# Gate and value of two more blocks by a seven-product scheme, with running sums carried between PSUM banks by ScalarE

## The chip, the cores and the metric

The kernel runs on one core of a Trainium2 chip. Its engines work side by side, each through its own queue, in the order of that queue: TensorE (PE: matmuls; PEld: its weight loads), VectorE (DVE), ScalarE (ACT), GpSimd (POOL) and SyncE (SP), which here issues the DMAs. The metric is the device time of one execution in microseconds (us); of the kernel before there are three runs, with a median of 913.91 us (913.44 to 915.89).

## The reference

Three stages follow each other on 2304 tokens of 512 numbers, all in fp32: attention within a window of 64 positions (4 sequences of 576, 8 heads of 64), then two gated feed-forward layers of width 1536. Cut to what is computed:

```python
attn = softmax(mask(q @ k.T / 8)) @ v          # rel in [0, 64)
x = attn.transpose(0, 2, 1, 3).reshape(2304, 512)
xn = x / sqrt(mean(x * x) + 1e-6) * rms_g      # layer 1
g = xn @ w_gate
x1 = (g * sigmoid(g) * (xn @ w_val)) @ w_out
gate = sigmoid(x1 @ w2_gate)                   # layer 2
out = (gate * (x1 @ w2_val)) @ w2_out
```

## The kernel before

**Tiles.** The tokens are cut into six blocks of 384 (`BLOCKS`). The width 1536 is cut into 12 groups `f` of 128, two of which share one weight tile: the tiles 0 to 11 of a layer are gate and value in turn, 12 to 17 are `w_out`. Each fp32 matrix is multiplied as three fp16 matmuls (high by high, high by low, low by high), and weights and activations are therefore split into a high and a low half first: ScalarE writes the high half, VectorE the low one (`w_split`, L312; `rms_split`, L543; `moe_h`, L598). The weights come in by 1 MB DMAs (`w_load`), their largest value is found (`w_max`, L237), they are converted (`w_conv`, L264 to L266) and split (L327, L329).

**Layer 1** (`l == 0` in the code) goes block by block and group by group: `moe_g` and `moe_v` each put 12 matmuls of 128x384 into one bank (L567; 4 slices of the 512 inputs, 3 matmuls each), `moe_h` splits the product, and `moe_o` (L627 to L629) adds its 12 matmuls to four banks of the output. Blocks 0 and 1 share a first stretch in which the weights are still being prepared; blocks 2 to 5 follow, each with its attention and its normalisation placed ahead of it by `place`.

**Layer 2** (`l == 1`) takes two blocks as a pair and uses Strassen's scheme in Winograd's form for gate and value. The inputs are seen as a 2x2 matrix of quadrants (two halves of the 512 inputs, two blocks) and the weights as one of 2x2 quadrants. Seven products of six matmuls (`product`, L737) take the place of eight. The sums of weight quadrants are made by `w_sums` (L303), the sums of input quadrants by `xform_items` (L696). In `moe_w` (L743) the results are put together: ScalarE copies one product out of its bank (L752), VectorE makes five additions with L741, each reading a bank, and two further products are added by TensorE itself into a bank that holds a product already. The output matmuls are L633 to L635.

**Order.** Every instruction gets a priority from `at` and `place`; the final order on each engine is then fixed by `arrange` (L1086) from a packed table, `ORDER` (L1041), with the scheduler's dependencies kept as semaphore waits. PSUM has eight banks: 0 to 3 hold outputs, 4 and 5 serve `moe_g` and `moe_v`, 4 to 7 serve `moe_w` (`BANKS_OF`).

## Time and profile before

| | |
|---|---|
| median of three runs | 913.91 us |
| the profiled execution, its own time | 915.78 us |
| its span, first to last instruction | 914.0 us |
| PE busy | 886.4 us (97%) |
| DVE busy | 634.2 us (69%) |
| ACT busy | 394.6 us (43%) |
| mean granted TensorE clock | 0.981 |

Busy time is the time in which an engine has an instruction under way. The span is 1.78 us shorter than the profiled execution's own time, which is 1.87 us above the median. By the timeline the matmuls of layer 1 begin at 51.86 us, the last matmuls of layer 1 and the first steps of layer 2 lie around 523 us, and the last matmul starts at 909.46 us.

### The profile page before, as it was taken

How to read it: one execution, taken by the hardware profiler on the slowest of the kernel's cores; microseconds unless marked ns; L12 is line 12 of the kernel's file. 1: busy time of each engine (PE TensorE's matmuls, PEld its weight loads, DVE VectorE, ACT ScalarE, POOL GpSimd, SP SyncE). 2: the span in 40 equal slices, each digit the busy share in tenths (PEclk: the TensorE clock that was granted, in tenths of full speed). 3: DMA queues.
4: the chain of work that ended last, by engine and by line, in shares of the span. 5: the costliest groups of instructions: out<-in, count | busy, mean ns of one | idle time of the engine just before them, and what ended most of it. 6: DMA issues, size and time to landing. Idle time of an engine off the chain costs nothing.

```text
span 914.0 us, 14970 instructions
## 1 busy us (share of the span) xinstructions
PE 886.4 (97%) x6120; PEld 527.9 (58%) x6120; DVE 634.2 (69%) x1209; ACT 394.6 (43%) x834; POOL 28.4 (3%) x37
## 2 busy tenths in 40 slices
PE   4699999999999999999999999999999999999998
PEld 3566665666666666666666655555555555555543
DVE  6999999798887689446789788657454644534440
ACT  5867546456553544432363554234223331323220
POOL 0000000000010001001000000000000000000000
PEclk7689999999999999999999999999999999999999
DMA  8752634312322163100021211000010000000001
GB/s 318 244 207 104 237 133 156 128 52 81 122 98 82 54 209 148 37 24 1 1 93 47 93 47 47 1 1 1 1 47 1 1 12 1 24 24 24 1 24 58
DMA packets 18789, 68.11 MB, mean 75 GB/s; under 512 B 2208, under 2 KB 2592, under 8 KB 13600
## 3 DMA queue, kind: packets, MB, share of 16 engines
q1 hardware_dynamic: 18720, 67.15, 20.5%
q8 instruction: 48, 0.79, 0.4%
q14 instruction: 21, 0.17, 0.1%
HBM read 62.43 MB, written 4.72 MB: 73 GB/s over the span
## 4 chain that ended last, share of the span: by engine, by line
PE 83%; DVE 11%; DMA 4%; issue 1%; ACT 1%; SPq 0%; POOL 0%; ACTq 0%
PE bank L737 27%; PE bank L567 23%; PE bank L635 5%; PE bank L634 5%; PE bank L633 5%; PE bank L627 4%; PE bank L629 4%; PE bank L628 4%; DVE wl L329 2%; PE bank L472 2%; DMA wl<-in_moe_w_val_dram 2%; PE bank L435 2%; DVE wmax L237 2%; DMA wl<-in_moe_w_gate_dram 1%; PE bank L402 1%; DVE wl L266 1%
## 5 line engine op out<-in xcount | busy, mean ns | idle before, releaser
L567 PE MATMUL bank<-xhl,wl 128*128 128x384 f16 x1728 | 297.3, 326 | 1.5 <-DVE th L581 1.1
L567 PEld LDWEIGHTS <-wl 128*128 128x128 f16 x1728 | 167.8, 98 | 112.1 <-issue 3.6
L737 PEld LDWEIGHTS <-wl 128*128 128x128 f16 x1512 | 148.0, 98 | 108.3
L737 PE MATMUL bank<-att,wl 128*128 128x384 f16 x1008 | 176.1, 326 | 0.0
L579 ACT ACTIVATE th<-bank,tg 128x384 f32<-128x384 f32 x72 | 41.6, 578 | 102.9 <-PE bank L567 68.8
L741 DVE TENSOR_TENSOR xhl<-xhl,bank 128x384 f32<-128x384 f32 x74 | 40.7, 552 | 61.3 <-PE bank L737 56.3
L627 PE MATMUL bank<-hh,wl 128*128 128x384 f16 x192 | 62.7, 326 | 0.0
L628 PE MATMUL bank<-hh,wl 128*128 128x384 f16 x192 | 62.6, 326 | 0.0
L629 PE MATMUL bank<-hh,wl 128*128 128x384 f16 x192 | 62.6, 326 | 0.0
L327 ACT ACTIVATE wl<-wl,isc 128x1024 f16<-128x1024 f32 (+1 forms) x42 | 48.5, 1162 | 17.2 <-DVE isc L246 10.2
L581 DVE SCALAR_TENSOR_TENSOR th<-th,bank 128x384 f32<-128x384 f32 x72 | 39.4, 548 | 22.6 <-ACT th L579 22.3
L592 DVE SCALAR_TENSOR_TENSOR th<-th,bank 128x384 f32<-128x384 f32 x72 | 39.4, 547 | 13.9 <-PE bank L567 13.3
L237 DVE TENSOR_REDUCE wmax<-wl 128x1 f32<-128x1024 f32 x36 | 43.6, 1213 | 5.5 <-DMA wl<-in_moe_w_val_dram 2.7
L264 ACT ACTIVATE wl<-wl 128x1024 f32<-128x1024 f32 x36 | 41.1, 1148 | 12.8 <-PE bank L567 3.7
L737 PE MATMUL bank<-wl 128*128 128x384 f16 x252 | 45.5, 326 | 0.0
L737 PE MATMUL bank<-wl,wl 128*128 128x384 f16 x252 | 45.4, 326 | 0.0
L418 ACT ACTIVATE sm<-sm,nm 128x128 f32<-128x128 f32 x96 | 37.3, 391 | 17.8 <-DVE nm L412 17.6
L633 PE MATMUL bank<-wl,xhl 128*128 128x512 f16 x111 | 42.1, 379 | 0.0
L634 PE MATMUL bank<-wl,xhl 128*128 128x512 f16 x111 | 42.1, 379 | 0.0
L635 PE MATMUL bank<-wl,xhl 128*128 128x512 f16 x111 | 42.1, 379 | 0.0
L629 PEld LDWEIGHTS <-wl 128*128 128x128 f16 x288 | 28.2, 98 | 18.8 <-DVE wl L329 0.2
L627 PEld LDWEIGHTS <-wl 128*128 128x128 f16 x288 | 28.2, 98 | 18.4 <-issue 1.0
(246 smaller groups left out, 1305.8 us busy)
## 6 DMA issues: line engine op xcount, KB each, us to landing
wl<-in_moe_w_out_dram SPq DMA_DIRECT2D x15, 1024.0 KB, 4.9
wl<-in_moe_w_val_dram SPq DMA_DIRECT2D x13, 1024.0 KB, 4.9
wl<-in_moe_w_gate_dram SPq DMA_DIRECT2D x12, 1024.0 KB, 5.0
vn<-in_v_dram SPq DMA_DIRECT2D x27, 256.0 KB, 3.5
att<-in_k_dram SPq DMA_DIRECT2D x13, 384.0 KB, 5.6
att<-in_q_dram SPq DMA_DIRECT2D x17, 256.0 KB, 5.2
out_dram<-vn SPq DMA_DIRECT2D x12, 256.0 KB, 2.1
out_dram<-sm SPq DMA_DIRECT2D x6, 256.0 KB, 2.3
```

Of the source, the lines that this page charges most:

```text
L237: V.tensor_reduce(out=r1[:, i:i + 1], in_=wraw(layer, j + i)[:, :, 1].bitcast(F32), axis=AX.X, op=ALU.max, apply_absolute_value=True)
L264: A.activation(out=y.bitcast(F32), in_=hi.bitcast(F32), func=AF.Prelu, scale=2.0 ** -112, alpha=-2.0 ** 32)
L327: A.activation(out=hi, in_=y, func=AF.Copy, scale=sc)
L567: T.matmul(pb[:, 0:n], lhsT=w_, rhs=x_, start=(c == 0), stop=(c == m - 1))
L579: A.activation(out=th[:, 0:n], in_=pg[:, 0:n], func=AF.Tanh, scale=sc)
L627: T.matmul(o[c][:, 0:n], lhsT=wh[:, cs], rhs=hi, start=st, stop=False)
L628: T.matmul(o[c][:, 0:n], lhsT=wh[:, cs], rhs=lo, start=False, stop=False)
L629: T.matmul(o[c][:, 0:n], lhsT=wl[:, cs], rhs=hi, start=False, stop=en)
L633: T.matmul(o[t], lhsT=h[:, 0, ts_], rhs=wh, start=st, stop=False)
L634: T.matmul(o[t], lhsT=h[:, 0, ts_], rhs=wl, start=False, stop=False)
L635: T.matmul(o[t], lhsT=h[:, 1, ts_], rhs=wh, start=False, stop=en)
L737: T.matmul(pb[:, 0:NMAX], lhsT=w_, rhs=x[:, t, kk], start=first and c == 0, stop=c == 5, skip_group_check=not first)
```

## The change

Blocks 4 and 5 of layer 1 (`PAIRED`) become a pair like those of layer 2: six steps `("W", 0, 2, s)` of seven products for gate and seven for value stand where 24 calls each of `moe_g` and `moe_v` stood, and the matmuls of L567 for them, 2 blocks x 12 groups x 24 matmuls = 576, become 6 steps x 2 x 7 products x 6 matmuls = 504. For it:

- the normalised blocks 4 and 5 stay in fp32 (no `rms_split`; the multiplication of 128x1536 in `rms_scale`, L541, becomes four of 128x384 that take the gain in), and `xform_items(0, 2)` makes their seven sums: four subtractions of 128x768 on VectorE, seven splits of 128x768 on both engines;
- the sums of layer 1's weight quadrants are made from the split weights, per tile: the high and low half are added back (`s_sum`, 128x1024), then the four sums of 128x256, then two splits (`s_hi`, `s_lo`), for 12 tiles;
- seven weight tiles of layer 2 (4 to 10) are now loaded twice: once early for `w_max`, once again for conversion; in all 47 instead of 40 weight loads.

In both layers `moe_w` puts the results together in another way: each gate or value of a step has three ScalarE copies (L809 after; two of them from one bank to another, where the following product is added on top) and two VectorE additions, where it had one copy and five additions.

```diff
+PAIRED = (4, 5)
...
+    def s_sum(s, m):
+        x, d = s_raw(m), wdst(0, 2 * s + m)
+        V.tensor_tensor(out=x[:, :, 1], in0=d[:, 0:1024], in1=d[:, 1024:2048], op=ALU.add)
+
+    def s_hi(s, m):
+        x, d, r = s_raw(m), wdst(0, 2 * s + m), s_form(s, m)
+        A.activation(out=r[:, 0:768], in_=x[:, 0:768, 0], func=AF.Copy, scale=0.25)
+        A.activation(out=d[:, 768:1024], in_=x[:, 768:1024, 1], func=AF.Copy, scale=0.25)
+
+    def s_lo(s, m):
+        x, d, r = s_raw(m), wdst(0, 2 * s + m), s_form(s, m)
+        V.scalar_tensor_tensor(out=r[:, 768:1536], in0=x[:, 0:768, 0], scalar=0.25, in1=r[:, 0:768], op0=ALU.mult, op1=ALU.subtract)
+        V.scalar_tensor_tensor(out=d[:, 1792:2048], in0=x[:, 768:1024, 1], scalar=0.25, in1=d[:, 768:1024], op0=ALU.mult, op1=ALU.subtract)
...
-            a = bank("w")
-            product(a, p, s, m, 0, 0, True)
+            def go(pb, a, b, first=False):
+                product(pb, l, p, s, m, a, b, first)
+
+            def copy(o, i):
+                A.activation(out=o[:, 0:NMAX], in_=i[:, 0:NMAX], func=AF.Copy)
+
+            a, e = bank("w"), bank("w")
+            go(a, 0, 0, True)
+            go(e, 6, 6, True)
             b = bank("w")
-            product(b, p, s, m, 5, 5, True)
-            u2 = take()
-            A.activation(out=u2, in_=a[:, 0:NMAX], func=AF.Copy)
-            add(u2, u2, b[:, 0:NMAX])
-            d = bank("w")
-            product(d, p, s, m, 4, 4, True)
-            u4 = take()
-            add(u4, u2, d[:, 0:NMAX])
-            e = bank("w")
-            product(e, p, s, m, 6, 6, True)
-            c22 = take()
-            add(c22, u4, e[:, 0:NMAX])
-            product(a, p, s, m, 1, 1, False)
...
+            copy(b, a)
+            go(b, 5, 5)
+            go(a, 1, 1)
+            c = bank("w")
+            copy(c, b)
+            go(c, 4, 4)
+            go(b, 2, 3)
+            x22, x21 = take(), take()
+            copy(x21, e)
+            add(x22, x21, c)
+            add(x21, x21, b)
+            go(c, 3, 2)
...
-    for b in range(DEFER, SKEW):
+    for b in range(DEFER, PAIRED[0]):
         gv(0, b, range(FC))
+    for s in range(NG):
+        main.append(("W", 0, 2, s))
+        if s:
+            oo(0, 4, [2 * s - 2, 2 * s - 1])
+    oo(0, 4, [10, 11])
+    oo(0, 5, range(FC))
...
 ORDER = (
-    'c-n1N2S8L;x}I~+T!yJkp$srX9~i(vdKG;tDE35*i7_VGly#p<Of-4xiZO9bdD$eIP1I+i8>6nSCbo?lD=P-22#6?k=pCfPG^X71MwuDz9h`E@DgQbD_'
+    'c-n1O30zdw{-57Dckb*A+pzDTvV$m~prB?V8foS7K9yVKQam*=%Oy*nOSzS%zWmeQ>`Cg&J#me+z%X+|kj;feLH5-FhFR`C@3PFyy<@YTbI<x)zQ6D9H'
```

The table `ORDER` is new from its first entry on. Three places of it follow; the names are tiles with their buffer number and the program's number, and a bracket names the engine or DMA queue whose semaphore is waited for.

**The start, on VectorE.** Before, from its third instruction; `nm` is a maximum of the attention scores, `wmax` that of a weight tile:

```order
L409 TENSOR_REDUCE nm_0_142<-bank_0_122 128x4 [waits PE_49]
L409 TENSOR_REDUCE nm_0_142<-bank_1_123 128x4 [waits PE_49]
L414 TENSOR_SCALAR nm_0_142<-nm_0_142 128x8 [waits DVE_49]
L265 TENSOR_SCALAR wl2_74<-wl2_74 128x1024 [waits DMAHW3_49]
L237 TENSOR_REDUCE wmax_0_390<-wl2_74 128x1
L270 TENSOR_REDUCE gam_0_114<-rg_77 128x1 [waits DMAHW6_49]
L266 SCALAR_TENSOR_TENSOR wl2_74<-wl1_73,wl2_74 128x1024 [waits DVE_49,Activation_49]
L192 TENSOR_SCALAR pgam_79<-gamr_0_116 128x1 [waits Pool_49]
L193 TENSOR_SCALAR pgam_79<-pgam_79 128x1 [waits DVE_49]
L409 TENSOR_REDUCE nm_1_180<-bank_2_160 128x4 [waits PE_49]
```

After:

```order
L412 TENSOR_REDUCE nm_0_143<-bank_0_123 128x4 [waits PE_49]
L412 TENSOR_REDUCE nm_0_143<-bank_1_124 128x4 [waits PE_49]
L417 TENSOR_SCALAR nm_0_143<-nm_0_143 128x8 [waits DVE_49]
L412 TENSOR_REDUCE nm_1_181<-bank_2_161 128x4 [waits PE_49]
L412 TENSOR_REDUCE nm_1_181<-bank_3_162 128x4 [waits PE_49]
L417 TENSOR_SCALAR nm_1_181<-nm_1_181 128x8 [waits DVE_49]
L238 TENSOR_REDUCE wmax_0_391<-wl2_74 128x1 [waits DMAHW5_49]
L266 TENSOR_SCALAR wl2_74<-wl2_74 128x1024
L422 TENSOR_SCALAR su_0_144<-su_0_144 128x8 [waits Activation_49]
```

The scores of the second pair (`nm_1`) come ahead of the first weight tile, whose `w_max` comes ahead of its conversion. SP issues the second pair's `k` and `q` ahead of the first weight tile too, where they came behind it.

**ScalarE, around the end of layer 1.** Before, in block 5's gate and value (L579 is the tanh of `moe_g`, L608 the high half of `moe_h`, L264 and L327 conversion and split of weights, L752 the copy and L781 the tanh of the first step of layer 2):

```order
L608 ACTIVATE hh_2_2311<-th_1_535 128x384 [waits DVE_49]
L752 ACTIVATE th_0_469<-bank_6_209 128x384 [waits DVE_49,Activation_49]
L579 ACTIVATE th_2_605<-bank_4_197,tg1_84 128x384 [waits PE_49]
L264 ACTIVATE wl1_73<-wl2_74 128x1024 [waits DMAHW5_49,PE_49]
L608 ACTIVATE hh_3_2399<-th_2_605 128x384 [waits DVE_49,PE_49]
L702 ACTIVATE wl1_73<-xhl_2_326,sx_1_5592 128x768
L781 ACTIVATE hh_0_2161<-bank_6_209,be_0_4910 128x384 [waits DVE_49,PE_49]
L327 ACTIVATE wl1_73<-wl2_74,isc_83 128x1024 [waits DVE_49]
```

After, in the paired blocks (L809 is the copy, L832 the tanh, L759 and L760 are the two lines of `s_hi`):

```order
L809 ACTIVATE bank_7_211<-bank_4_198 128x384 [waits DVE_49,PE_49]
L832 ACTIVATE vn_1_359<-hh_3_2394,tgs_87 128x384 [waits DVE_49,Activation_49]
L832 ACTIVATE th_1_536<-bank_5_204,tgs_87 128x384 [waits PE_49]
L759 ACTIVATE wl2_74<-wl2_74 128x768 [waits DVE_49]
L330 ACTIVATE wl1_73<-wl2_74,isc_83 128x768
L809 ACTIVATE bank_5_204<-bank_7_211 128x384 [waits DVE_49,PE_49]
L330 ACTIVATE wl1_73<-wl2_74,isc_83 128x1024
L809 ACTIVATE hh_3_2394<-bank_6_210 128x384 [waits DVE_49,PE_49,Activation_49]
L760 ACTIVATE wl1_73<-wl2_74 128x256 [waits DVE_49]
L809 ACTIVATE bank_4_198<-bank_6_210 128x384 [waits DVE_49,PE_49]
```

Four copies, three of them between banks, stand between splits of weights that wait for VectorE.

**ScalarE, in layer 2, where the second pair begins.** Before (L790 is the split of the gated product, L702 that of an input sum):

```order
L752 ACTIVATE th_0_469<-bank_6_209 128x384 [waits DVE_49,PE_49]
L790 ACTIVATE th_2_605<-wl2_74,hs2_88 128x384 [waits DVE_49]
L790 ACTIVATE xhl_1_263<-xhl_1_263,hs2_88 128x384 [waits DVE_49]
L781 ACTIVATE wl2_74<-wl2_74,be_0_4910 128x384
L781 ACTIVATE wl2_74<-bank_6_209,be_1_5613 128x384 [waits PE_49,Activation_49]
L752 ACTIVATE xhl_1_263<-bank_7_210 128x384 [waits PE_49]
L702 ACTIVATE att_76<-xhl_3_521,sx_2_6329 128x768
```

After (L809 the copy, L832 the tanh, L850 the split, L708 that of an input sum):

```order
L832 ACTIVATE xhl_2_327<-bank_4_198,be_1_5728 128x384 [waits PE_49]
L809 ACTIVATE bank_4_198<-bank_6_210 128x384 [waits PE_49,Activation_49]
L832 ACTIVATE xhl_3_522<-bank_5_204,be_1_5728 128x384 [waits PE_49]
L809 ACTIVATE bank_5_204<-bank_4_198 128x384 [waits PE_49,Activation_49]
L832 ACTIVATE xhl_2_327<-xhl_2_327,be_1_5728 128x384 [waits DVE_49]
L708 ACTIVATE att_76<-xhl_1_264,sx_2_6434 128x768
L809 ACTIVATE xhl_3_522<-bank_7_211 128x384 [waits PE_49]
L850 ACTIVATE wl2_74<-wl2_74,hs2_89 128x384
L832 ACTIVATE xhl_2_327<-xhl_2_327,be_1_5728 128x384
L809 ACTIVATE bank_6_210<-bank_7_211 128x384 [waits DVE_49,PE_49]
L809 ACTIVATE bank_5_204<-bank_6_210 128x384 [waits DVE_49,PE_49]
L809 ACTIVATE wl2_74<-bank_4_198 128x384 [waits PE_49,Activation_49]
```

Where two copies out of a bank stood, six copies stand, four of them into a bank, and for those TensorE waits.

## Rows read from the trace of the kernel before

**Rows 1.** The page's head: busy time by engine, and TensorE in 40 slices.
```profile
PE 886.4 (97%) x6120; PEld 527.9 (58%) x6120; DVE 634.2 (69%) x1209; ACT 394.6 (43%) x834; POOL 28.4 (3%) x37
PE   4699999999999999999999999999999999999998
```

**Rows 2.** Windows: stretch, length, busy (instructions) of PE, PEld, DVE, ACT, POOL, clock, DMA.
```profile
0.00:52.00 52.00, 31.27 (x361) 23.70 (x362) 42.15 (x109) 34.75 (x94) 2.95 (x8) 0.67 0.77 274
52.00:150.00 98.00, 97.28 (x765) 61.94 (x764) 96.14 (x201) 61.89 (x124) 4.58 (x9) 1.00 0.45 162
150.00:300.00 150.00, 148.01 (x1222) 92.68 (x1220) 127.16 (x225) 79.34 (x191) 10.18 (x8) 1.00 0.29 103
300.00:523.00 223.00, 223.00 (x1611) 137.74 (x1610) 160.40 (x292) 97.00 (x215) 10.07 (x11) 1.00 0.20 69
52.00:523.00 471.00, 468.29 (x3594) 292.35 (x3593) 383.70 (x717) 238.23 (x527) 24.82 (x28) 1.00 0.28 99
523.00:910.00 387.00, 386.84 (x2168) 211.88 (x2166) 208.33 (x385) 121.05 (x215) 0.59 (x1) 1.00 0.05 18
```

**Rows 3.** Waits of PE from 52 us on: for whom, us, times, longest.
```profile
PE bank L435 <- DVE sm L427: 1.2, 1, 1.2
PE bank L567 <- DVE th L581: 1.1, 2, 0.6
PE bank L567 <- DVE xhl L549: 0.2, 1, 0.2
```

**Rows 4.** The chain that ended last, one piece: start, us, what.
```profile
604.50 1.95 PE bank L737 x12
```

**Rows 5.** Groups by line and shape: busy us, mean ns, idle before.
```profile
L741 DVE TENSOR_TENSOR xhl<-xhl,bank 128x384 f32<-128x384 f32 x74 | 40.7, 552 | 61.3 <-PE bank L737 56.3 <-ACT hh L790 2.1 <-ACT xhl L790 1.5
L307 DVE TENSOR_TENSOR wl<-wl 128x256 f32<-128x256 f32 x12 | 5.0, 420 | 0.0
L703 DVE SCALAR_TENSOR_TENSOR att<-xhl,sx,att 128x768 f16<-128x768 f32 x14 | 14.1, 1010 | 0.0
L706 DVE TENSOR_TENSOR xhl<-xhl,xhl 128x768 f32<-128x768 f32 x9 | 8.6, 950 | 0.0
L237 DVE TENSOR_REDUCE wmax<-wl 128x1 f32<-128x1024 f32 x36 | 43.6, 1213 | 5.5 <-DMA wl<-in_moe_w_val_dram 2.7 <-DMA wl<-in_moe_w_gate_dram 2.4 <-DMA wl<-in_moe_w_out_dram 0.4
L329 DVE SCALAR_TENSOR_TENSOR wl<-wl,isc,wl 128x1024 f16<-128x1024 f32 x21 | 26.8, 1278 | 3.0 <-ACT wl L327 2.8
L541 DVE TENSOR_TENSOR att<-att,xhl 128x1536 f32<-128x1536 f32 x4 | 7.0, 1757 | 0.1
L752 ACT ACTIVATE xhl<-bank 128x384 f32<-128x384 f32 x19 | 9.3, 489 | 53.0 <-PE bank L737 53.0
L790 ACT ACTIVATE xhl<-xhl,hs 128x384 f16<-128x384 f32 x18 | 10.9, 608 | 19.6 <-DVE xhl L786 18.6 <-DVE hh L791 1.0
```

**Rows 6.** Timeline of DVE: start, us, line, two neighbours.
```profile
642.28 0.61 DVE L791 SCALAR_TENSOR_TENSOR wl<-wl,hs,wl 128x384 f16<-128x384 f32 x1
642.81 0.55 DVE L786 SCALAR_TENSOR_TENSOR wl<-wl,bank 128x384 f32<-128x384 f32 x1
```

**Rows 7.** Timeline: three products in a row, and the copy of the first.
```profile
578.68 3.09 PE L737 MATMUL bank<-att,wl 128*128 128x384 f16 x18
579.86 0.49 ACT L752 ACTIVATE xhl<-bank 128x384 f32<-128x384 f32 x1 [3.96 <-PE bank L737]
581.61 0.38 PE L633 MATMUL bank<-wl,th 128*128 128x512 f16 x1
```

**Rows 8.** Timeline of DVE and PE: a late release in the first stretch.
```profile
69.19 0.55 DVE L581 SCALAR_TENSOR_TENSOR th<-th,bank 128x384 f32<-128x384 f32 x1
69.79 2.11 PE L567 MATMUL bank<-xhl,wl 128*128 128x384 f16 x12 [0.58 <-DVE th L581]
```

**Rows 9.** Timeline of PE and DVE: the start.
```profile
11.98 1.99 PE L402 MATMUL bank<-att 64*64 64x128 f32 x32 [5.10 <-DMA att<-in_q_dram]
10.24 0.70 DVE L265 TENSOR_SCALAR wl<-wl 128x1024 int32<-128x1024 int32 x1 [1.81 <-DMA wl<-in_moe_w_val_dram]
```

More of the change, by code (lines that the diff above doesn't have):

```diff
@@ L310, in w_sums @@
         V.tensor_tensor(out=a21, in0=a12, in1=s2, op=ALU.subtract)
+    def w_sums(j):
+        sums(wraw(1, j).bitcast(F32))
     def w_split(layer, j, half):
@@ L539, in rms_scale @@
         x = xf[blk][:, :, 0:n]
-        E = V
-        E.tensor_tensor(out=x, in0=x, in1=sq[:, 2:3, 0:n].to_broadcast([P, KC, n]), op=ALU.mult)
+        if blk in PAIRED:
+            for c in range(KC):
+                V.scalar_tensor_tensor(out=x[:, c], in0=x[:, c], scalar=cg[:, c:c + 1], in1=y, op0=ALU.mult, op1=ALU.mult)
+        else:
+            V.tensor_tensor(out=x, in0=x, in1=sq[:, 2:3, 0:n].to_broadcast([P, KC, n]), op=ALU.mult)
     def rms_split(blk):
@@ L574, in moe_g @@
         pg = bank("gv")
-        mm3(pg, [(wgv(l, 0, kk, f), xs[kk]) for kk in range(KC)], n)
+        mm3(pg, [(wgv(0, kk, f), xs[kk]) for kk in range(KC)], n)
         th = xp.tile([P, NMAX], F32, tag="th", name="th", bufs=3)
@@ L722, in xform_items, with s_home @@
         ]
-        if p:
-            fs.append(lambda: x1_c(p))
-        return [(("xf", p, i), f) for i, f in enumerate(fs)]
+        if l:
+            fs.insert(0, lambda: x1_scale(p))
+            if p:
+                fs.append(lambda: x1_c(p))
+        return [(("xf", l, p, i), f) for i, f in enumerate(fs)]
+    sreg = {}
+    def s_home(s):
+        if s not in sreg:
+            if s in (2, 3):
+                a = xp.tile([P, 2, KC, NMAX], F16, tag="xhl", name="xhl", bufs=SKEW).rearrange("p a k n -> p (a k n)")
+            else:
+                k = (28, 34, None, None, 28, 34)[s]
+                a = wl2[:, k * KIB:(k + 6) * KIB]
+            sreg[s] = a
+        return sreg[s]
@@ L727, in take, with h5_home, product @@
+    h5 = {}
+    def h5_home(f):
+        s, i = divmod(f, 2)
+        if s == 1:
+            return abuf("sm", 0)[:, 0:NMAX]
+        if s in (2, 3):
+            if "x" not in h5:
+                h5["x"] = six()
+            return h5["x"][:, 2 * (s - 2) + i]
+        o = {0: (40, 54), 4: (28, 29.5), 5: (31, 32.5)}[s][i]
+        o = int(o * KIB)
+        return wl2[:, o:o + 2 * NMAX].bitcast(F32)
     def take():
         return room.pop(0)
-    def product(pb, p, s, m, a, b, first):
-        w, x = wdst(1, 2 * s + m), xform(p, b)
-        c = 0
+    def product(pb, l, p, s, m, a, b, first):
+        w, x = wdst(l, 2 * s + m), xform(l, p, b)
+        lo = 1792 if l else 1024
+        if not l and a > 3:
+            w, a, lo = s_form(s, m), a - 4, 768
@@ L733, in product @@
         for kk in range(2):
             o = a * 256 + kk * P
-            wh, wl = w[:, o:o + P], w[:, 1792 + o:1792 + o + P]
-            for w_, t in ((wh, 0), (wh, 1), (wl, 0)):
-                T.matmul(pb[:, 0:NMAX], lhsT=w_, rhs=x[:, t, kk], start=first and c == 0, stop=c == 5, skip_group_check=not first)
-                c += 1
+            wh, wl = w[:, o:o + P], w[:, lo + o:lo + o + P]
+            for n, (w_, t) in enumerate(((wh, 0), (wh, 1), (wl, 0))):
+                T.matmul(pb[:, 0:NMAX], lhsT=w_, rhs=x[:, t, kk], start=first and kk == n == 0, stop=kk == 1 and n == 2, skip_group_check=not first)
@@ L961, in fused_kernel @@
-        place(lst, w0 - 1, pos["W", 1, 0, 4], post)
-        place(xform_items(1), pos["W", 1, 0, 4], w[1] - CO, post)
-        place(xform_items(2), pos["W", 1, 1, 3], w[2] - CO, post)
+        y0 = pos["W", 0, 2, 0]
+        w = [pos["W", 1, p, 0] for p in range(NB // 2)]
+        lst = [load(j) for j in (0, 1, 2, 3)] + conv_pair(1, 0) + conv_pair(1, 2)
+        lst += [load(12), load(13)] + conv(1, 12) + [load(14)] + conv(1, 13) + conv(1, 14)
+        for j in (4, 5, 6, 7, 8, 9, 10, 11, 15, 16, 17):
+            lst += pre_max(j)
@@ new lines, in fused_kernel, with again, after @@
+        lst.append((("ws2",), w_l2_scale))
+        lst.append((("tgs",), lambda: V.tensor_scalar(out=tgs, in0=tg1, scalar1=8.0, scalar2=None, op0=ALU.mult)))
+        place(lst, pos["O", 0, 0, FC - 1], pos["GV", 0, 3, 3], post)
+        place(s_items(0) + s_items(1), pos["GV", 0, 3, 4], y0, mid)
+        place(xform_items(0, 2), y0, y0 + 1, mid)
+        def again(*js):
+            return [load(j) for j in js] + interleave(*[conv_rest(1, j) for j in js])
+        def after(l, b, f, lst):
+            place(lst, pos[l, 0, b, f] + 1, pos[l, 0, b, f] + 2, mid)
```

276 lines of the change are left out of this document (142 added, 134 removed).

## The prediction, as it was put on record

> **What bounds the kernel now.** I read the page's head first: TensorE is busy for 886.4 us of 914.0, VectorE for 69%, ScalarE for 43% [rows 1]. A mean says little of stages, so the windows come next. From 300 to 523 us TensorE is busy for all of 223.00 us, in layer 2 (523 to 910) for 386.84 of 387; from 52 to 300 it loses 2.7 us [rows 2]. The waits say who holds it up there: 1.2, 1.1 and 0.2 us, all for VectorE [rows 3]. Busy matmul rows can hide small holes, since they overlap (18 in a row end 0.16 us after the next instruction began [rows 7]); so I look at the distance. Twelve matmuls of 128x384 take 1.95 us on the chain, 0.1625 us each [rows 4], and three products of six, 18 matmuls, start at 578.68 and are followed by the next instruction at 581.61: 2.93 us, 0.163 each [rows 7]. There are no holes. From 52 us on the kernel's time is the sum of its matmuls plus 2.7 us.
>
> In that first stretch (52 to 150 us) VectorE is full as well, 96.14 of 98 us, while TensorE still gets 97.28 [rows 2]. So the order in the queues can feed two full engines at once; that matters below. The clock granted to TensorE is 1.00 in all of these windows, the 2.4 GHz level, with TensorE running without a break; only the first 52 us have 0.67.
>
> **What goes.** 576 matmuls become 504, of the same shape: 72 x 0.1625 = 11.7 us less on the engine that sets the time. Nothing covers them: every one is on the path.
>
> **What is added on VectorE.** One instruction occupies the engine for less than its row says: a 0.61 us one is followed by the next after 0.53, so I take 0.08 us off each row [rows 6]. In layer 1, by [rows 5]:
> - adding halves back, 12 of 128x1024: no such form in the trace; the reduce of that size (1.213) and the split (1.278) give 1.13 to 1.20; I take 1.13, as it does no scaling: 13.6 us
> - sums of weight quadrants, 48 of 128x256: 0.34 each, 16.3
> - their low halves, 12 of 128x768 at 0.93 and 12 of 128x256 (between the 0.34 of a sum and the 0.53 of a 128x384 split [rows 6]; 0.39): 15.8
> - input sums, 7 x 0.93 and 4 x 0.87: 10.0
> - two additions per gate or value, 24 x 0.47: 11.3; a scaled low half in place of a plain one, 24 x 0.06: 1.4
> - normalising: two of 128x1536 go (1.68 each), eight of 128x384 come and eight alike of `rms_split` go: -3.4
>
> The sum is 65.0 us. VectorE had 383.7 us of work in the 471 us from 52 to 523 [rows 2]; it would have 448.7 in 459.3, or 97.7%. That is as full as the first stretch, but for nearly five times as long. In layer 2 the opposite: 36 gates and values lose three additions each, 108 x 0.47 = 50.8 us of 208.3, which buys nothing, since TensorE has no wait there.
>
> How long VectorE's fullness makes TensorE wait, the trace bounds from two sides. At the rate of the first stretch (0.72 us in 98) 459.3 us would cost 3.4, against the 2.7 lost now: +0.7. At that of 150 to 300 us, the worst (1.99 in 150), 6.1: +3.4. All waits gone would be -2.7, which nothing suggests. I take **+2.0**.
>
> By the Trainium skill (Perfetto Trace Analysis, Identifying the Most-Contended Engine) a TensorE is not to be judged by busy matmul time but by arithmetic done and by the busy share of its weight loads, and the engine with the highest occupancy is to be relieved first. Here the weight loads are busy for 58% and VectorE for 69% [rows 1], so by that rule the change relieves the wrong engine and loads the right one, and the time would not fall; the sum would be that of the first rival. The trace does not agree: a weight load lies within the 0.1625 us of a matmul three times as wide as it, so its share cannot near 100% here, and the matmuls stand without holes [rows 4, 7].
>
> **What is added on ScalarE.** 144 copies of 0.49 us where 36 were; in the paired blocks also the high halves of those splits, of about VectorE's durations. It gets to about 270 us of 459 in layer 1 and 156 of 387 in layer 2: no bound. But two copies in three now feed TensorE: the next product in that bank waits. How tight that is follows from [rows 7]. The first of three products starts at 578.68 and its last matmul ends about 0.98 + 0.16 us later, at 579.82; the copy runs from 579.86 to 580.35; the third product starts at 580.63. With one product between, 0.28 us are to spare, and VectorE's additions (0.55) leave 0.22. By the order, 22 products after have only one product between them and the one that their copy or addition reads (16 behind copies, 6 behind additions); 18 have that before (2 behind ScalarE, 16 behind additions), and no wait of TensorE came of any of them [rows 3]. A copy into a bank is not in the trace; its nearest row is the copy out of one, 0.489, and from above the 0.608 of a split, which would still fit. So I cost the copies at **0**, covered by the product between. If that cover goes, each of the 22 is late by what stands ahead of it in ScalarE's queue: one instruction of 0.60 less the 0.28 to spare, 0.32, or 7.0 us in all. Behind a waiting copy stand tanh and splits, for which VectorE and then TensorE's banks wait.
>
> **What is moved.** At the start SP issues the second pair's `q` and `k` (0.66 MB) ahead of the first weight tile. TensorE's wait of 5.10 us for that `q` [rows 9] shrinks, but it is not what counts: VectorE is busy for 42.15 of the first 52 us, from 10.24 on almost without a break, and the first product of layer 1 waits for it. Ahead of that product its queue holds eight reduces of weight tiles in place of seven (+1.13) and four small instructions fewer (-0.2): +0.9. From below: the 1.81 us that VectorE idles before its first weight tile could go, as the second pair's scores stand there now: -1.8. From above: the weights come 0.66 MB later, 2.4 us at the 274 GB/s of the first 52 us [rows 2]: +3.3. I take **+1.0**, near the count of its queue. The seven further weight loads of 1 MB find queues that are 20% busy (300 to 523 us) [rows 2]: nothing.
>
> **The sum**: -11.7 + 2.0 + 0 + 1.0 = -8.7 us. The profiled execution took 915.78 us by its own time (span 914.0) and would take 907.1; it lay 1.87 above the median of 913.91, so for the median I predict **905.2 us**. What is late next is the same TensorE, which then waits for VectorE in all of layer 1.
>
> **The rivals.**
> *VectorE becomes the bound of layer 1: slower.* 448.7 us of work must fit. The point from which it decides is 448.7/471 = 95.3%: if its queue, in which each instruction waits its turn behind others that wait for ScalarE or a DMA, reaches less than that, the stage is longer than now. At 93% it takes 482.5 us, +11.5, with +1.0 at the start: 926 us. For it: 150 to 300 us, where VectorE was at 85% and TensorE waited nonetheless [rows 2, 3]; a release that came 0.05 us before TensorE ran on, 0.58 us late, because a reduce stood ahead of it [rows 8]; after, ScalarE's copies stand behind splits that wait for VectorE, so that a delay reaches TensorE in two ways. Against it: the 98.1% of the first stretch. Chance 9%, for 914 to 930.
> *The copies eat the gain.* The 7.0 us above: 913.91 - 8.7 + 7.0 = 912.2, no change that can be told. For it: a bank now passes from TensorE to ScalarE and back in one chain, and ScalarE's queue holds waits ahead of copies. Against it: none of 18 such places cost anything. Chance 8%.
> *The gain in full*: -11.7 and the start at -1.8, no further waits: 900.4. It is the low end of the forecast, 8% beyond it.
>
> **How the numbers follow.** The forecast has 75%. Its own bounds are -11.7 + 0.7 - 1.8 = -12.8 and -11.7 + 3.4 + 3.3 = -5.0, so 901.1 to 908.9. I take the range up to 911.0, half-way into the copies' case: **901 to 911**. About 0.3% (2.7 us) is what a measurement of this kernel can tell from no change, so faster means below 911.2. Faster: the forecast, the full gain and part of the copies, 86%. Within: most of the copies and the near end of VectorE's case, 7%. Slower: VectorE's case, 7%.
>
> **What would show it.** Right: TensorE with 6048 matmul rows, 72 fewer, still 0.1625 us apart; busy for nearly all of layer 2; waits from 52 us to the end of layer 1 of 3 to 6 us, for VectorE's `th` and low halves; VectorE at about 97% of layer 1 and about 157 us in layer 2; the copies into banks near 0.49 us; the first product of layer 1 around 53 us. Wrong: many waits of TensorE for L809; VectorE's idle time in layer 1 above 5% with TensorE waiting; sums of 128x1024 that take well over 1.2 us; a granted clock below 1.00 after 62 us.

## The result, and the profile after

The kernel after takes 905.23 us (median of four runs, 904.74 to 905.88), the kernel before 914.23 us in its four runs (913.44 to 915.89): a ratio of 0.990, with a 95% interval from 0.988 to 0.992. That is 9.0 us less, where I had forecast 905.2 us. The number came out. Of its terms the start is not borne out, and the waits have about the size forecast for another reason than the one given.

The head of the page after, busy time by engine and TensorE in 40 slices, answers to [rows 1]:

```profile
PE 873.1 (97%) x6048; PEld 519.5 (58%) x6048; DVE 641.0 (71%) x1228; ACT 454.6 (50%) x965; POOL 30.8 (3%) x40
PE   4699999999999999999999999999999999999998
```

72 matmuls are gone, ScalarE has 60 us more, VectorE hardly more in all. By stage it is another matter. The windows after (columns as in [rows 2]; layer 1 begins at 50.50 us and ends around 511):

```profile
0.00:51.00 51.00, 29.73 (x362) 22.47 (x363) 42.11 (x106) 35.08 (x95) 4.90 (x9) 0.77 0.73 275
51.00:150.00 99.00, 98.00 (x768) 62.18 (x768) 96.82 (x206) 63.49 (x135) 3.17 (x8) 1.00 0.44 160
150.00:300.00 150.00, 147.50 (x1249) 93.57 (x1248) 139.29 (x245) 79.60 (x196) 13.60 (x16) 1.00 0.46 171
300.00:511.00 211.00, 209.45 (x1497) 128.44 (x1496) 197.39 (x387) 119.53 (x253) 8.52 (x6) 1.00 0.13 46
51.00:511.00 460.00, 454.95 (x3510) 284.18 (x3510) 433.49 (x836) 262.62 (x582) 25.29 (x30) 1.00 0.30 111
511.00:899.00 388.00, 388.00 (x2177) 212.89 (x2176) 165.40 (x289) 156.23 (x288) 0.64 (x1) 1.00 0.07 26
```

VectorE is busy for 433.5 of 460 us in layer 1 (94.2%), where it had 383.7 of 471 [rows 2], and for 165.4 in layer 2, where it had 208.3. TensorE now loses 5.0 us in layer 1 and nothing in layer 2. For whom, the waits of TensorE from 51 us on say (waited for, us, times, longest; the five largest, a sixth is 0.2 us), beside [rows 3]:

```profile
PE bank L577 <- DVE th L590: 1.7, 3, 0.8
PE bank L577 <- DVE th L600: 1.2, 1, 1.2
PE bank L796 <- DVE att L709: 0.9, 1, 0.9
PE bank L438 <- DVE sm L430: 0.6, 1, 0.6
PE bank L529 <- DVE xhl L528: 0.5, 1, 0.5
```

All for VectorE, none for the copies of L809. The groups of the added work (columns as in [rows 5]: L755 adds the halves back, L764 is a low half of 128x768, L799 an addition that reads a bank, L809 the copy from bank to bank):

```profile
L755 DVE TENSOR_TENSOR wl<-wl 128x1024 f32<-128x1024 f16 x12 | 14.6, 1221 | 0.1
L764 DVE SCALAR_TENSOR_TENSOR wl<-wl 128x768 f16<-128x768 f32 x8 | 7.6, 951 | 0.6 <-ACT wl L759 0.6
L799 DVE TENSOR_TENSOR xhl<-xhl,bank 128x384 f32<-128x384 f32 x26 | 14.3, 552 | 34.3 <-PE bank L796 28.7 <-ACT wl L832 4.0 <-ACT wl L850 1.1
L809 ACT ACTIVATE bank<-bank 128x384 f32<-128x384 f32 x96 | 45.7, 476 | 121.3 <-PE bank L796 99.2 <-DVE xhl L840 8.0 <-DVE th L840 3.0
```

The start of a run varies by itself. So I also compare, in the profiled executions, the stretch from the first gate matmul of layer 1 to the start of the last matmul. It is 857.60 us before (51.86 to 909.46) and 848.57 after, where the first gate matmul starts at 50.50 and the last row of TensorE's timeline is this:

```profile
899.07 0.38 PE L638 MATMUL bank<-wl,xhl 128*128 128x512 f16 x1
```

The matmuls that went are 72 x 0.1625 = 11.7 us, and 2.7 of them came back as further waits: the waits listed from there on grow by about as much, from 2.5 us [rows 3] to 5.1. The two profiled spans differ by more than 9.03 us, by 10.8: the first gate matmul came 1.36 us earlier, which is not shown to be a gain (below), and behind the start of the last matmul 0.4 us less followed. The latter goes with the change: it is 4.12 to 4.13 us in all eleven traces of kernels with the change and 4.54 to 4.55 in the three without. What makes it was not tried.

### The profile page after: what moved, and what is told of

The parts are those of the page before. It is cut to its first block, busy times and chain, and to the rows that moved or that the text cites. A ratio compares the mean times of both kernels' runs of the same rounds, so it can differ in the third digit from the quotient of the medians.

```text
span 903.2 us, 14978 instructions
## 1 busy us (share of the span) xinstructions
PE 873.1 (97%) x6048; PEld 519.5 (58%) x6048; DVE 641.0 (71%) x1228; ACT 454.6 (50%) x965; POOL 30.8 (3%) x40
## 4 chain that ended last, share of the span: by engine, by line
PE 78%; DVE 15%; DMA 4%; issue 1%; ACT 0%; POOL 0%; SPq 0%; DVEq 0%; ACTq 0%
PE bank L796 36%; PE bank L577 11%; PE bank L637 5%; PE bank L638 5%; PE bank L636 5%; PE bank L628 4%; PE bank L630 4%; PE bank L629 4%; DVE wmax L238 2%; DVE wl L332 2%; DMA wl<-in_moe_w_gate_dram 2%; DMA wl<-in_moe_w_out_dram 1%; PE bank L405 1%; PE bank L477 1%; DVE wl L267 1%
## 5 line engine op out<-in xcount | busy, mean ns | idle before, releaser
L796 PEld LDWEIGHTS <-wl 128*128 128x128 f16 x1944 | 190.2, 98 | 137.2 <-issue 1.2
L796 PE MATMUL bank<-att,wl 128*128 128x384 f16 x1440 | 252.6, 326 | 0.9 <-DVE att L709 0.9
L577 PE MATMUL bank<-xhl,wl 128*128 128x384 f16 x1152 | 197.4, 326 | 3.2 <-DVE th L590 1.7
L577 PEld LDWEIGHTS <-wl 128*128 128x128 f16 x1152 | 112.0, 98 | 77.5 <-issue 5.1
L809 ACT ACTIVATE bank<-bank 128x384 f32<-128x384 f32 x96 | 45.7, 476 | 121.3 <-PE bank L796 99.2
L589 ACT ACTIVATE th<-bank,tg 128x384 f32<-128x384 f32 x48 | 27.7, 576 | 44.8 <-PE bank L577 34.1
L796 PE MATMUL bank<-wl,wl 128*128 128x384 f16 x252 | 45.2, 326 | 0.0
L840 DVE SCALAR_TENSOR_TENSOR xhl<-xhl,bank 128x384 f32<-128x384 f32 x18 | 9.9, 553 | 42.7 <-PE bank L796 42.7
L628 PE MATMUL bank<-wl,wl 128*128 128x384 f16 x120 | 39.2, 327 | 0.0
L629 PE MATMUL bank<-wl,wl 128*128 128x384 f16 x120 | 39.1, 326 | 0.0
L630 PE MATMUL bank<-wl,wl 128*128 128x384 f16 x120 | 39.1, 326 | 0.0
L630 PEld LDWEIGHTS <-wl 128*128 128x128 f16 x288 | 28.2, 98 | 18.6
L628 PEld LDWEIGHTS <-wl 128*128 128x128 f16 x288 | 28.1, 98 | 18.6 <-issue 1.0
L799 DVE TENSOR_TENSOR xhl<-xhl,bank 128x384 f32<-128x384 f32 x26 | 14.3, 552 | 34.3 <-PE bank L796 28.7
```

The lines of the kernel that those rows point to most:

```text
L577: T.matmul(pb[:, 0:n], lhsT=w_, rhs=x_, start=(c == 0), stop=(c == m - 1))
L628: T.matmul(o[c][:, 0:n], lhsT=wh[:, cs], rhs=hi, start=st, stop=False)
L629: T.matmul(o[c][:, 0:n], lhsT=wh[:, cs], rhs=lo, start=False, stop=False)
L630: T.matmul(o[c][:, 0:n], lhsT=wl[:, cs], rhs=hi, start=False, stop=en)
L796: T.matmul(pb[:, 0:NMAX], lhsT=w_, rhs=x[:, t, kk], start=first and kk == n == 0, stop=kk == 1 and n == 2, skip_group_check=not first)
L809: A.activation(out=o[:, 0:NMAX], in_=i[:, 0:NMAX], func=AF.Copy)
```

## The experiments

Each kernel below the first was timed in five rounds beside the kernel before. "Difference" is the median less that of the kernel before in the same runs; "stretch" is the time from the first gate matmul to the last matmul in the profiled execution, and in brackets against 848.57 (against 857.60 for the two kernels made from the one before). A stretch is that of one execution, and some of it is chance: at 281.35 us the kernel after has a hole of 0.8 us, a wait for L590, that seven of the ten kernels made from it do not have, though three of the seven differ from it only behind that place; and ahead of the first matmul that a_wide changes, it is 1.1 us faster than the kernel after. Differences of about 1 us in this column therefore say nothing by themselves. Where I say below at which place time is lost, I have compared the starts of the same matmuls in two traces.

| kernel | median | difference | stretch |
|---|---|---|---|
| after | 905.23 | -9.0 | 848.57 |
| b_narrow | 906.54 | -8.5 | 849.57 (-8.0) |
| a_wide | 915.92 | +0.9 | 858.80 (+10.2) |
| a_light | 902.24 | -12.8 | 845.32 (-3.3) |
| a_half | 909.39 | -5.2 | 852.03 (+3.5) |
| a_heavy | 916.57 | +1.6 | 860.06 (+11.5) |
| b_heavy | 921.38 | +6.2 | 864.39 (+6.8) |
| a_copy512 | 904.12 | -10.5 | 848.90 (+0.3) |
| a_copy2 | 909.14 | -5.5 | 853.37 (+4.8) |
| a_adds2 | 911.74 | -3.4 | 854.44 (+5.9) |
| a_poolsums | 930.47 | +15.9 | 875.04 (+26.5) |
| a_norm | 910.75 | -4.4 | 852.40 (+3.8) |
| a_order | 904.93 | -9.4 | 846.66 (-1.9) |

### The saving, given back: a_wide

```diff
-                T.matmul(pb[:, 0:NMAX], lhsT=w_, rhs=x[:, t, kk], ...)
+                z = 467 if not l and t == 0 else NMAX
+                c = (2 * t + kk) * NMAX
+                T.matmul(pb[:, 0:z], lhsT=w_, rhs=x[:, c:c + z], ...)
```

> The kernel after, with 336 of the 504 gate and value matmuls of the paired blocks of layer 1 widened from 384 to 467 columns, the further columns being used by nothing: 336 x 83 columns, some 11.8 us more on TensorE, the saving of the change given back. My theory (TensorE sets the time in the paired blocks): 905.2 + 11.8 = 917.0, less up to 2.4 us of the waits that VectorE's fullness costs, as it then has 11.8 us more: 914.6 to 917. Rival (VectorE has become the bound of the paired blocks): TensorE then only waits less, 905 to 907.

The stretch grew by 10.2 us for 11.8 us of matmuls, and the median is 0.9 us above the kernel before. TensorE's time in the paired blocks is on the path, as forecast. Of the missing 1.6 us, 1.1 lie ahead of the first widened matmul (373.17 us), where the two kernels are alike; from there on the kernel is 11.3 us slower, and a wait for L709 is 0.4 us shorter.

### The saving alone, in the kernel before: b_narrow

```diff
-                T.matmul(pb[:, 0:n], lhsT=w_, rhs=x_, start=(c == 0), stop=(c == m - 1))
+                w = z if z and c else n        # z = 332 in blocks 4 and 5
+                T.matmul(pb[:, 0:w], lhsT=w_, rhs=x_[:, 0:w], start=(c == 0), stop=(c == m - 1))
```

> The kernel before, with nothing changed but that the gate and value matmuls of blocks 4 and 5 (all but the first of each twelve) take 332 columns in place of 384: 528 x 52 columns, at 0.1625 us for 384 some 11.6 us less on TensorE, nothing added on VectorE or ScalarE. Columns 332 to 383 of these blocks are left incomplete. My theory (the time is the sum of the matmuls, and what the change adds on VectorE costs TensorE some 2.7 us of waits): 914.2 - 11.6 = 902.6, from 902 to 903.5, so some 2.5 us below the kernel after. Rival (a shorter TensorE part waits by itself, whatever is added on VectorE): 904.5 to 906, as the kernel after.

My expectation missed: 8.0 of the 11.6 us came out, though nothing was added anywhere. Most of the rest are new holes: by the distance of its matmuls, ten of them, 3.0 us in all, stand behind the first narrowed one, two of the ten in layer 2. The waits of TensorE name VectorE, which frees the banks; of the eight times listed here, five lie in blocks 4 and 5 (433 to 495 us):

```profile
PE bank L568 <- DVE th L593: 1.1, 4, 0.3
PE bank L568 <- DVE th L582: 1.0, 4, 0.3
```

A shorter product finds its bank not yet free. So some 3 us of waits need not come of what the change adds: a faster TensorE in an order that was not made for it has them too.

### VectorE lighter and heavier: a_light, a_half, a_heavy

In a_light the sums of weight quadrants take 32 of 256 columns and layer 2's largest values 128 of 1024 (the splits behind the sums read those 32 columns 24 times, so that they keep their size). In a_heavy each addition of halves is made twice, in a_half only those of the gate tiles:

```diff
-        V.tensor_tensor(out=x[:, :, 1], in0=d[:, 0:1024], in1=d[:, 1024:2048], op=ALU.add)
+        twice(V.tensor_tensor, out=x[:, :, 1], in0=d[:, 0:1024], in1=d[:, 1024:2048], op=ALU.add)
```

> The kernel after with less work on VectorE in layer 1: the 48 sums of weight quadrants take 32 columns in place of 256 (about 0.28 us less each, 13 us; the sums of weights are then wrong), and the largest value of layer 2's 18 weight tiles is taken over 128 of 1024 columns (about 1 us less each, 18 us). Some 31 us less, 402 of 460 us in place of 433. My theory (VectorE's fullness costs TensorE about 2.4 us more waits than before): TensorE's waits after 51 us fall from 4.9 to about 2.5 us, and the time to 902.5 to 903.5. Rival (the waits come of the places of single instructions in VectorE's queue, not of its total): 904.5 to 905.5, the same waits.

> The kernel after, with each of the 12 additions of halves (128x1024) on VectorE made twice in a row, with the same result: 12 x 1.14 = 13.7 us more on VectorE, 447 of 460 us or 97.2%, which is the fullness that I had predicted for the kernel after. My theory (two full engines can be fed at once, at a few us of waits): 906 to 909.5. Rival (VectorE bounds layer 1 from 95.3% on): what is above that is paid in full, 447/0.953 = 469 in place of 460, +9 or more: 914 or above.

> The kernel after, with six of the 12 additions of halves (those of the gate tiles) made twice in a row, with the same result: 6.8 us more on VectorE, half of what cost 10.6 us. My theory by now (VectorE is the bound of the stretch from 150 us on as soon as it is fuller than in the kernel after, so that most of its further work is paid): +4.5 to +6 us against the kernel after. Rival (there is some room left, and the time jumps behind it): 0 to +2.

My expectation for a_light held in the main: the waits fall to 2.5 us, the time is a little below the range. Of the 3.3 us in its stretch, 1.2 lie at 51 and 281 us, at holes that most of the other kernels do not have either. My expectation for a_heavy fell: its rival had said +9 or more, and it is +11.5. a_half lies between, at +3.5, a little under what I had expected by then. One window over layer 1 of each, a_heavy's first:

```profile
51.00:523.00 472.00, 457.87 (x3512) 284.07 (x3510) 447.66 (x846) 262.22 (x581) 25.71 (x30) 1.00 0.30 108
```

a_half:

```profile
51.00:515.00 464.00, 456.24 (x3512) 284.18 (x3511) 440.05 (x840) 262.05 (x581) 25.12 (x30) 1.00 0.31 110
```

a_light:

```profile
51.00:508.00 457.00, 454.42 (x3511) 284.08 (x3509) 407.44 (x834) 261.27 (x581) 25.29 (x30) 1.00 0.31 112
```

Subtract VectorE's busy time (that of the third engine) from the length: it idles for 49.6 us in a_light, 26.5 in the kernel after, 24.0 in a_half and 24.3 in a_heavy. More work does not fill these last 24 us, and the kernel after stands 2.5 us above them. That reads like a floor below which VectorE's idle time cannot go in this order, but these runs do not show that the floor is what costs the time. In a_heavy TensorE's lost time comes in single waits, and 5.0 of the 11.5 us stand close behind a doubled addition, at 287.81, 298.44, 334.29 and 373.48 us. The second of these places (the second addition, the next instruction of VectorE, TensorE):

```profile
296.70 1.23 DVE L756 TENSOR_TENSOR wl<-wl 128x1024 f32<-128x1024 f16 x1
297.84 0.55 DVE L590 SCALAR_TENSOR_TENSOR th<-th,bank 128x384 f32<-128x384 f32 x1
298.44 2.11 PE L577 MATMUL bank<-xhl,wl 128*128 128x384 f16 x12 [0.83 <-DVE th L590]
```

Whether fullness or place sets the price needs the same load where VectorE has room. That is the next run.

### The same load on a VectorE with room: b_heavy

The kernel before takes the largest value of 12 tiles of layer 2 twice in a row, by the same `twice`.

> The kernel before, with the largest value of the 12 gate and value tiles of layer 2 taken twice in a row, with the same result: 12 x 1.13 = 13.6 us more on VectorE in layer 1, as much as cost the kernel after 10.6 us. VectorE gets to 397 of 471 us there, 84%. My theory (what an addition to VectorE costs hangs on how full it is): 0 to +1.5 us against the kernel before. Rival (each further instruction holds up those behind it, however full the engine is): +5 to +11.

This fell to the rival's side too: +6.8 us. VectorE has 14.3 us more to do in layer 1 and idles for 80 us there, at 83%. Windows of this kernel, all of layer 1 first (columns as in [rows 2]):

```profile
52.00:530.00 478.00, 471.50 (x3605) 293.07 (x3598) 398.03 (x729) 238.84 (x528) 24.83 (x28) 1.00 0.28 98
158.00:161.50 3.50, 0.80 (x7) 0.57 (x6) 3.43 (x7) 1.21 (x1) 0.86 (x1) 0.99 0.43 145
161.50:165.00 3.50, 3.50 (x14) 1.95 (x12) 3.09 (x4) 1.20 (x2) 0.00 (x0) 0.52 0.37 154
```

And rows of its timeline at two places, TensorE at the first, VectorE's added reduce and TensorE at the second (start, us, line, and in brackets the idle time before it):

```profile
160.95 0.63 PE L441 MATMUL bank<-ident,sm 128*128 128x128 f32 x4 [2.70 <-DVE sm L433]
161.69 0.53 PE L634 MATMUL bank<-wl,wl 128*128 128x384 f16 x1
...
484.91 1.22 DVE L232 TENSOR_REDUCE wmax<-wl 128x1 f32<-128x1024 f32 x1
486.65 1.62 PE L573 MATMUL bank<-xhl,wl 128*128 128x384 f16 x9 [1.27 <-DVE th L587]
```

At the first, a wait of 2.70 us (1.24 in the kernel before) for a normalised attention tile behind the added reduces, and 3.5 us at a granted clock of 0.52 behind it, with rows of 0.53 in place of 0.33 us: together 3.0 of the 6.8 us. Most of the rest, 3.6 us, lies at eight places between 246 and 511 us, most of all at the second one shown, where TensorE waits 1.27 us for the instruction that follows an added reduce. So a further instruction is dear on an engine with room as well, if TensorE waits for one that stands right behind it: 0.5 us for each us added, as in a_half, where VectorE is at 94.8%. How full VectorE is does not by itself explain that price.

### The copies: a_copy512, a_copy2

```diff
-                A.activation(out=o[:, 0:NMAX], in_=i[:, 0:NMAX], func=AF.Copy)
+                w = 512 if o.tensor.name.startswith("bank") else NMAX      # a_copy512
+                A.activation(out=o[:, 0:w], in_=i[:, 0:w], func=AF.Copy)
...
+                if o.tensor.name.startswith("bank"):                       # a_copy2
+                    twice(A.activation, out=o[:, 0:NMAX], in_=i[:, 0:NMAX], func=AF.Copy)
```

> The kernel after, with the 96 copies from bank to bank taking 512 columns in place of 384; the further columns are used by nothing. By the 594 ns of the 128x512 copies out of a bank against 476 ns, each is some 0.12 us longer. My theory (0.28 us to spare where only one product lies between): no change, within 1 us of the kernel after, which by the 915.0 us of the kernel before in the first runs of experiments would be at about 906. Rival (the copies are paid): 16 tight places x 0.12 = 1.9 us, or, if each copy is on the path, 96 x 0.12 = 11.3 us.

> The kernel after, with each of the 96 copies from bank to bank made twice in a row, with the same result: the bank is ready some 0.42 us later and ScalarE has 40 us more. My theory (0.28 us to spare): in the 16 tight places 0.14 us too much each, 2.2 us, and with what VectorE's full queue makes of it +2 to +5 us against the kernel after. Rivals: the copies have far more room than I worked out, no change; or every copy is on the path, +40 us.

Both as expected. 583 ns in place of 476 for each copy cost 0.3 us in the stretch; a second copy cost 4.8. Its timeline shows a tight place (PE, then ScalarE twice, then the next PE):

```profile
391.24 3.02 PE L802 MATMUL bank<-att,wl 128*128 128x384 f16 x16
392.09 0.47 ACT L754 ACTIVATE bank<-bank 128x384 f32<-128x384 f32 x1 [2.00 <-PE bank L802]
392.59 0.47 ACT L756 ACTIVATE bank<-bank 128x384 f32<-128x384 f32 x1
```

The second copy starts 0.50 us after the first. Sixteen matmuls at 0.1625 us would be done in 2.76 us with the overlap of the last; they take 3.02, since the product that needs this bank begins 0.26 us late. So 0.50 - 0.26 = 0.24 us were to spare, where I had worked out 0.28. From 386 us on 18 holes of over 0.15 us stand in TensorE's timeline. One of them, at 386.44, is in the kernel after too; the other 17 make 4.6 us, and half of them are about 0.26 us. I had counted 16 such places in the order.

### Layer 2's additions: a_adds2

```diff
+                twice(V.tensor_tensor, out=x22, in0=x21[:, 0:NMAX], in1=c[:, 0:NMAX], op=ALU.add)   # layer 2
+                twice(V.tensor_tensor, out=x21, in0=x21[:, 0:NMAX], in1=b[:, 0:NMAX], op=ALU.add)
```

> The kernel after, with the 72 additions of layer 2 (L799) made twice in a row, one in two with a wrong result: 72 x 0.47 = 34 us more on VectorE there, 199 of 392 us in place of 165, two thirds of what the change took from it in layer 2. My theory (what was taken from VectorE in layer 2 bought nothing, since TensorE has no wait there): 0 to +1.5 us against the kernel after, the latter for banks that come free 0.47 us later. Rival (the lighter VectorE of layer 2 is a part of the gain): +4 us or more.

Outside my expectation, and by the number on the rival's side: +5.9 us. They lie in layer 2; what this run loses at 253 us in layer 1, which is not edited, it gets back at 282, where it lacks the 0.8 us hole of the kernel after. It is no matter of how full VectorE is, which is busy for 198 of 393 us there. The timeline at one place (VectorE's two additions, TensorE's product):

```profile
514.96 0.56 DVE L754 TENSOR_TENSOR th<-th,bank 128x384 f32<-128x384 f32 x1 [2.07 <-PE bank L802]
515.55 0.55 DVE L756 TENSOR_TENSOR th<-th,bank 128x384 f32<-128x384 f32 x1
...
516.16 1.14 PE L802 MATMUL bank<-att,wl 128*128 128x384 f16 x6 [0.33 <-DVE th L756]
```

The product waits for the second addition, 0.49 us by the distance of its matmuls, and starts 0.06 us after its end. With one addition it would have been free at 514.96 + 0.55 + 0.06 = 515.57, and the matmuls ahead end their turn at 515.67: 0.10 us to spare, not the 0.22 that I had for additions. The run doubles a latency with a load, so that it does not show what the lighter VectorE of layer 2 is worth by itself.

### Work moved to other engines: a_poolsums, a_norm

The moved instructions keep about the times that they had; the lines that place them in the new queue are left out here.

```diff
-        sums(wraw(1, j).bitcast(F32))
+        sums(wraw(1, j).bitcast(F32), G)                                    # a_poolsums
...
-NORM_ACT = set()
+NORM_ACT = {(p, e) for p in range(6, 18) for e in range(2) if True}         # a_norm
```

> The kernel after, with the 48 sums of layer 2's weight quadrants (L307 to L310) on GpSimd in place of VectorE, at about the times that they have now. VectorE loses 48 x 0.34 = 16 us, some 12 of them in layer 1, where 13.7 us more of work (the additions made twice) cost 10.6 us and 31 us less gave some 4 back. My theory (VectorE's fullness costs the kernel after about 2.5 us): 1.5 to 3 us faster than the kernel after. Rival (GpSimd is so much slower, or in the way of VectorE's own reads, that the splits and the additions behind it come late): no gain, or some us slower.

> The kernel after, with the 24 multiplications that normalise the attention from about 130 us on (L430, 128x512) made by ScalarE, as four of 128x128 each. VectorE loses 24 x 0.61 = 14.6 us in layer 1, ScalarE gets some 26 more and stands at about 289 of 460 us there. My theory (what VectorE loses comes back at the rate of the run with 31 us less, 0.1 to 0.2 us each, since the kernel after stands at the bend): 1.5 to 2.5 us faster than the kernel after. Rival (ScalarE's four instructions come later than VectorE's one did, and the transposes wait for them): no gain, or up to 3 us slower.

Both lost. In a_norm VectorE is 9 us lighter between 150 and 300 us, and TensorE waits for ScalarE's normalising instead, 1.6 us by the waits. By the distance of its matmuls it loses more there: the attention's transposes (L444), four for each tile that ScalarE now normalises in four pieces, take 4.8 us longer than in the kernel after, while the gate and value matmuls and the ones of the normalisation (L529 in the kernel after) lose 1.9 less. In a_poolsums one of GpSimd's sums takes 0.60 to 0.85 us in 34 of 48 cases and up to 1.82 in the others, on VectorE 0.42, and at about 197 us they came late; VectorE then waited 7.14 us for a split, and TensorE for VectorE; a second wait of 6.85 us follows at 229 us. The first row is from a_norm, the second from a_poolsums:

```profile
171.56 1.21 PE L444 MATMUL bank<-ident,sm 128*128 128x128 f32 x4 [0.49 <-ACT sm L429]
204.15 1.09 PE L440 MATMUL bank<-ident,sm 128*128 128x128 f32 x4 [7.22 <-DVE sm L432]
```

Neither had its order found anew, so they show only that such a move is not free where it is put.

### Two instructions moved: a_order

In the kernel after, two of TensorE's holes stand behind these rows (VectorE at both places, then TensorE):

```profile
249.95 1.22 DVE L238 TENSOR_REDUCE wmax<-wl 128x1 f32<-128x1024 f32 x1 [1.08 <-DMA wl<-in_moe_w_gate_dram]
251.09 0.54 DVE L600 SCALAR_TENSOR_TENSOR th<-th,bank 128x384 f32<-128x384 f32 x1
382.77 0.95 DVE L712 TENSOR_TENSOR xhl<-xhl,xhl 128x768 f32<-128x768 f32 x1
...
251.68 2.11 PE L577 MATMUL bank<-xhl,wl 128*128 128x384 f16 x12 [1.18 <-DVE th L600]
384.71 0.97 PE L796 MATMUL bank<-att,wl 128*128 128x384 f16 x5 [0.92 <-DVE att L709]
```

L600 had its inputs and stood behind a reduce that waited for its DMA; L709 stood behind an input difference (L712) for which TensorE did not wait. Both go one step ahead:

```diff
+MOVED = [(469, 468), (715, 713)]        # places in VectorE's order
```

> The kernel after with two instructions of VectorE moved ahead in its queue, and nothing else: the multiplication L600 for which TensorE waits at 251.68 us goes ahead of the largest value (L238) that waits there for its DMA, and the low half L709 for which TensorE waits at 384.71 us goes ahead of an input difference (L712). No work is added or taken away. My theory by now (the waits come of single places of VectorE's queue, and an order found for the durations mends or makes them): the holes of 1.35 and 1.09 us go or shrink to 0.2, and from the first to the last matmul of layers 1 and 2 it takes 846.3 to 846.9 in place of 848.57 us; the time is 1.7 to 2.3 us below the kernel after, about 903. Rival (VectorE's total sets the waits): they turn up again some instructions later, 848 to 849.

The stretch is 846.66 us, as expected, 1.9 below the kernel after. At the first place (TensorE, then VectorE):

```profile
249.29 4.06 PE L577 MATMUL bank<-xhl,wl 128*128 128x384 f16 x24
249.62 0.55 DVE L600 SCALAR_TENSOR_TENSOR th<-th,bank 128x384 f32<-128x384 f32 x1
250.37 1.22 DVE L238 TENSOR_REDUCE wmax<-wl 128x1 f32<-128x1024 f32 x1 [0.20 <-DMA wl<-in_moe_w_gate_dram]
```

24 matmuls without a hole. But part of what was won was lost again close behind. The two places gave 2.3 us; 0.3 came back at 256.70 us, where TensorE waits longer for L590, and 0.7 at two places at which TensorE now waits for a copy into a bank. At the first of them the copy stands behind a split of ScalarE (L708) that waits for the input difference, which now comes later (ScalarE, then TensorE at both places):

```profile
383.78 0.84 ACT L708 ACTIVATE att<-xhl 128x768 f16<-128x768 f32 x1 [0.35 <-DVE xhl L712]
384.53 0.47 ACT L809 ACTIVATE bank<-bank 128x384 f32<-128x384 f32 x1
385.05 2.11 PE L796 MATMUL bank<-att,wl 128*128 128x384 f16 x12 [0.17 <-ACT bank L809]
389.81 1.14 PE L796 MATMUL bank<-att,wl 128*128 128x384 f16 x6 [0.21 <-ACT bank L809]
```

So the two moves are worth about 1.2 us. The other 0.7 of the 1.9 us are the hole at 281 us, which this run lacks as six others do: the number came out as expected in part by luck, and the rival, by which the holes turn up again some instructions later, holds for almost half of them. The median (904.93 us, ratio 0.990 with an interval from 0.988 to 0.992) is not measurably below that of the kernel after.

## Why the prediction was right, and where it was not

**The 72 matmuls: right.** 6048 rows, and 11.7 us of them in the stretch. a_wide shows the price from the other side.

**The copies at 0: right,** and for the reason given. No wait of TensorE for L809; one product between covers a copy with 0.24 us to spare (a_copy2), and the count of tight places fits. The rival in which the copies eat the gain needed a copy longer by 0.3 us or more, or one that comes late; a_order shows that its mechanism exists, with a copy behind a split that waits for VectorE, though in the kernel after it cost nothing. For the additions the reason held less well: 0.10 us to spare at the place looked at, not 0.22.

**The waits, +2.0: the size right, the reason not.** They came to 2.7 us, inside +0.7 to +3.4, and most of them for the forecast's `th` and low halves. But I had put VectorE at 448.7 us of work in layer 1, 97.7%, and held that to cost a few us, since the first stretch has both engines full. The term that failed is that load: it is 433.5 us, so that one of the signs that I had named for being wrong came, VectorE idle for over 5% of layer 1 (26.5 of 460 us, 5.8%) with TensorE waiting. The prices were not the cause: over both layers the lengths of VectorE's rows grew by 15.6 us, and mine come to 15.1 before the 0.08 us taken off each row. But some 12 us of the work that I had put into layer 1 stand behind 511 us in the new order, where layer 2 has room (165.4 us there, not 157.5), and as VectorE's rows stand closer, more of their ends overlap (58.7 us in layer 1, before 46.3), which busy time counts once.

So the inference from the first stretch, that two full engines can be fed for five times as long at the same rate of waits, was not put to the test by the kernel after. The runs speak against it where work is added in place: a_heavy has 447.7 us on VectorE, and its stretch is 11.5 us longer. That looks like the first rival, which named 95.3% as the point from which VectorE decides; a_heavy stands at 94.8%, the kernel after at 94.2%. But b_heavy paid 0.5 us for each us added at 83%, so that these runs do not show fullness to be the cause; in all of them the added instruction makes a later one late for which TensorE waits. b_narrow has 3 us of new waits with nothing added. What the waits of the kernel after come of, beyond the instructions named in the list, and what an order found for a_heavy's load would make of it, stays open.

By the Trainium skill (Perfetto Trace Analysis, Identifying the Most-Contended Engine) the engine with the highest occupancy is to be relieved first. The prediction set that rule aside for TensorE's weight loads, whose share is still 58% beside matmuls without holes; the other measure that the rule names for TensorE, the arithmetic done, it named and did not work out, so that the rule was not shown to speak against the change. For VectorE in layer 1 after, the runs bear it out in one direction only: adding to it costs 0.5 to 0.8 us for each us, taking 26 us from it (a_light) gives back at most 3.3.

**The start, +1.0: not borne out, and not settled.** The eight reduces ahead of the first product are there, but the profile after has the first gate matmul 1.36 us earlier, not 1.0 later. In the ten kernels made from the one after, with the same start, it stands anywhere from 49.47 to 52.51 us (with the kernel after itself a median of 51.2), in the three executions of the kernel before and its two variants at 50.34, 51.86 and 52.23. The difference of the kernels, if there is one, is smaller than that scatter, and +1.0 was worked out from a single sample on one side.

**Layer 2: right as far as it shows.** TensorE is busy for 388.0 of 388 us, as before. That VectorE's 43 us less bought nothing there fits, but a_adds2 could not show it cleanly.

**Why the time fits nevertheless:** -11.7 + 2.7 = -9.0 in the stretch, and 0.4 less behind the last matmul; the medians differ by 9.0, with an interval of about 7.6 to 10.8. The forecast had -8.7, with waits 0.7 too cheap, a start of +1.0 that no trace shows, and nothing for the end. That it came within 0.3 us is in part luck.

## What to carry to other kernels

In a kernel whose order is fixed, ask of an added instruction who stands right behind it and who waits for that, before asking how full the engine is: 14 us more on VectorE cost 6.8 us at 83% (b_heavy) and 11.5 at 94.8% (a_heavy). An edit in place is dearer than work whose order was found anew; the change raised VectorE's busy time in layer 1 by 50 us at 2.7. So test a suspected bound by adding as well as by taking away, and at a second load, and look at which places the time is lost before calling it a matter of load. And follow a mended hole further down: of the 2.3 us that two moved instructions gave, 1.0 came back.
